# Attention, a dense FFN and routed experts on one core: moving a fourth tile's gather and transposes, and joining two short scatters

## The chip, the cores and the metric

One core of a Trainium2 chip runs the whole program in one launch. The metric is the device time of that launch in microseconds (us). Engines by the names of the profile: PE (TensorE, matmuls and transposes), PEld (its weight loads), DVE (VectorE), ACT (ScalarE), POOL (GpSimd), SP (SyncE, which here only issues transfers). ACT and POOL issue transfers too; every indirect transfer (gather or scatter by a list of row numbers) is POOL's.

## The reference

Three stages, float32 in and out:

```
x   = attention(q, k, v)            # 4 batches, 8 heads, 512 local + 32 global positions, window 32
x   = relu(x @ w_in)**2 @ w_out     # (2176, 512) -> 2048 -> 512
out = moe2(x):
    compute = x @ w_skip > 0
    e_idx   = argmax(x[compute] @ w_gate)            # one of 8 experts
    gate    = softmax(x[compute] @ w_gate)[e_idx]
    y[mask of e] = gate * (relu(x[mask] @ w1[e]) @ w2[e])   # 512 -> 1024 -> 512
    out = x, and out[compute] = x + y
```

Only the third stage bears on the change. How many tokens an expert has is known only on the chip.

## The kernel before, in words

**Routing.** While the FFN runs, `route` gives each token a slot in its expert's list. Rows of x and the gate factor are stored in `x2d` (513 numbers a row), rows of x alone in `out`. `slot_rows` (L795) makes two integer tables: `gidx`, the row to gather for each slot, and `sidx`, the row of `out` to write (out of bounds for an empty slot). A column of 128 slots is one tile; tile (e, j) is expert e's j-th.

**A tile's work.** `gather(e, j)` (L882) is an indirect DMA of 128 rows into a buffer `xg`. `prepare(e, j)` (L888) is four PE transposes (`etr`), an ACT cast and a DVE subtraction, which leave the rows transposed as a high and a low part. `expert_tile(e, j)` (L897) is a generator of nine steps. Steps 0 to 3 are the first product in two halves (L912 to L914), each followed by its relu; after each half four transposes (`ertr`). Steps 4 to 7 are the second product, two of eight slices a step (L927 to L929, 6 matmuls of 128x512 a step, 24 in all). Step 8 is a DVE operation (L950) that multiplies by the gate and adds the token rows from `xg`. Then the indirect DMA (L954) scatters the result to `out`. All scatters write `out`, and each waits until the scatter before it has landed. The result's buffer (`"xt"`) is one.

**Order.** Each engine runs its instructions in the order in which they are emitted, and so does each of the queues of SP, ACT and POOL. The last part of the FFN and the first tiles of expert 0 follow a table written by hand, `TAIL` (L41): `X` and `Y` are steps of tiles (0, 0) and (0, 1); `g02`, `g10`, `g20` are gathers; `p02` is `prepare(0, 2)`; `z1`, `z2` transpose 32 rows of experts 1 and 2; `W` and `w` fetch expert weights on ACT's and SP's queue; `N` loads counts into registers. Weights come in parts of 512 KB, eight an expert (numbers 8e to 8e + 7).

**The branches.** `more(0, 2)` (L1258) runs tile (0, 2) if expert 0 has over 256 tokens. It emits the gather of (0, 3) at its head and `prepare(0, 3)` at step 5, and then branches on 384. On these data expert 0 has between 257 and 384 tokens: (0, 3) is gathered and transposed and never used. Expert 3 has four tiles, (3, 2) and (3, 3) as a pair; `more(3, 1)` emits their gathers at its head and their transposes at steps 5 and 6.

**The short form.** Experts 1 and 2 (`FEW`) have at most 32 tokens each, so `few` is taken (L1324). `rest_tile` (L1020) computes 32 tokens with plain fp32 weights: first product (L1029), relu, transposes, second product (L1048), four DVE operations of 32x128 (L1058) into a result tile (`"xt"` for expert 1, `"x2"` for expert 2), and a scatter of 32 rows (L1063). Both run interleaved. The branch first emits on SP the weight parts 23 to 28 (`fetch_expert`, L831; 23 is the last of expert 2, 24 to 31 are expert 3's), and ACT's first work in it is the cast of part 24 (L839). A part's transfer waits for its buffer, and for the semaphore that the eighth transfer before it used. `run` (L1304) then goes through experts 3 to 7: at step 5 of an expert's first tile `prepare(e, 1)`, at step 6 (`U0`) `prepare(e + 1, 0)`; its `later` list puts expert 2's DVE operations and scatter into steps 0 and 1 of tile (3, 0). An expert's next gathers stand at steps 2 and 3 (`AHEAD`).

Of the kernel before, what the change touches and what calls it, by code (L numbers as in the profile page):

```python
# [11 lines left out]
I32 = mybir.dt.int32  # L12
# [28 lines left out]
TAIL = """  # L41
    r W r w w T T s r s T T c T s T T r T T s r C T W w s O T W T C C T T W c C T W p00 c p01 T c T X w W X w t Z t
    X w X t X Y W t X X X t S Y W X w Y g02 Y N g10 g20 Y N N Y N W W X Y N N p02 N
    Y Y W Y Y W z1 z2
"""

WARM = 8
# [7 lines left out]
def attention_ffn_routed_experts(  # L55
# [22 lines left out]
    nc = tc.nc  # L78
    B, H, SL, D = q_l.shape
    SG = q_g.shape[2]  # L80
    P = 128
    S = SL + SG
    NTOK, DM = out.shape
# [31 lines left out]
    def sb(tag, bufs, shape, name, dtype=F32):  # L115
        return spool.tile(shape, dtype, tag=tag, bufs=bufs, name=name + arm[0])
# [765 lines left out]
    def gather(e, j, gi):  # L882
        nc.gpsimd.indirect_dma_start(  # L883
            out=gathered(e, j), out_offset=None, in_=x2d, in_offset=bass.IndirectOffsetOnAxis(ap=gi, axis=0),
            bounds_check=NTOK - 1, oob_is_err=False,
        )
# [130 lines left out]
        rest[e] = rest_in[-1][:, z]  # L1017
        nc.scalar.copy(rest[e], tr[:, :, 0:SEG])

    def rest_tile(e, j, si, in_arm, o_tag):  # L1020

        x, fw = rest[e], F // NQ
        xg = gathered(e, j)[0:SEG]
        parts_in = [est[e * NPE + i] for i in range(NPE)]
        h = inner(in_arm, 0, f"eh_rest{e}")[:, 0:fw]
        for k in range(KD):
            for c in range(NQ):
                fb, at = divmod(c * fw, DM)
                nc.tensor.matmul(  # L1029
                    h[SEG * c:SEG * (c + 1), :], lhsT=x[:, k, :],  # L1030
                    rhs=parts_in[fb * (KD // 2) + k // 2][:, k % 2, at:at + fw],
                    start=(k == 0), stop=(k == KD - 1),
                )
        r = sb("sm", 2, [P, S], f"er_rest{e}")[:, 0:fw]
        nc.scalar.activation(r, h, AF.Relu)
        yield
        tr = pair(f"ertr_rest{e}")
        nz = fw // P
        for z in range(nz):
            nc.tensor.transpose(tr[:, z, :], r[:, z * P:(z + 1) * P], ident)  # L1040
        g = sb("pT", 2, [P, 4, P], f"eg_rest{e}")[:, 0:nz, :]
        nc.vector.tensor_copy(g, tr[:, 0:nz, :])
        yield
        y = ps.tile([P, DM], F32, tag="x2", bufs=2, name=f"y_rest{e}{arm[0]}")[:, 0:P]
        for f in range(KE):
            c, z = divmod(f, nz)
            for d in range(NQ):
                nc.tensor.matmul(  # L1048
                    y[SEG * d:SEG * (d + 1), :], lhsT=g[:, z, SEG * c:SEG * (c + 1)],
                    rhs=parts_in[NPE - KE // 2 + f // 2][:, f % 2, d * P:(d + 1) * P],  # L1050
                    start=(f == 0), stop=(f == KE - 1),
                )
        yield
        shape, bufs = {"xt": ([P, 3 * BLK], 1), "x2": ([P, ROW], 2)}[o_tag]
        o = sb(o_tag, bufs, shape, f"eo_rest{e}")[0:SEG, 0:DM]
        for d in range(NQ):
            cols = slice(d * P, (d + 1) * P)
            nc.vector.scalar_tensor_tensor(  # L1058
                out=o[:, cols], in0=y[SEG * d:SEG * (d + 1), :], scalar=xg[:, DM:DM + 1], in1=xg[:, cols],
                op0=ALU.mult, op1=ALU.add,  # L1060
            )
        yield
        nc.gpsimd.indirect_dma_start(  # L1063
            out=out, out_offset=bass.IndirectOffsetOnAxis(ap=si[0:SEG], axis=0), in_=o, in_offset=None,
            bounds_check=NTOK - 1, oob_is_err=False,
        )
        yield

    UNROLL = 5
# [3 lines left out]
    with tc.manual_schedule():  # L1073
# [103 lines left out]
        def slot(idx, e, j):  # L1177
            c = e * TPE + j
            return idx[:, c:c + 1]
# [13 lines left out]
        for what in TAIL.split():  # L1193
            if what == "T":
                next(ffn, None)
            elif what in "XY":
                j = "XY".index(what)
                if j not in early:
                    early[j] = expert_tile(0, j, first_slots[1][:, j:j + 1])
                next(early[j], None)  # L1200
            elif what in "rst":
                if what not in route_gens:
                    route_gens[what] = route(*outs["g"])
                next(route_gens[what])
            elif what in "Cc":
                convert_expert(converted[0], nc.vector if what == "C" else nc.gpsimd)
                converted[0] += 1
            elif what in "Ww":
                fetch_expert(fetched[0], nc.scalar if what == "W" else nc.sync)
                fetched[0] += 1  # L1210
            elif what == "O":
                open_places()
            elif what == "S":
                slot_rows(gidx, sidx, 0, NSLOT)
                nc.vector.tensor_tensor(
                    out=sizes[:, E:E + 1], in0=count[:, FEW[0]:FEW[0] + 1], in1=count[:, FEW[1]:FEW[1] + 1], op=ALU.max
                )
                nc.vector.tensor_copy(cnt, sizes)
            elif what == "N":
                load_count(to_load.pop(0))  # L1220
            elif what == "Z":
                convert_expert(converted[0], low_only=True)
            elif what[0] == "z":
                prepare_rest(int(what[1]), 0)
            elif what[0] in "gp":
                e, j = map(int, what[1:])
                if what[0] == "g":
                    gather(e, j, slot(gidx, e, j))
                else:
                    prepare(e, j)  # L1230
# [27 lines left out]
        def more(e, j):  # L1258

            if j == UNROLL:  # L1260
                with tc.For_i(UNROLL, (n_tok[e] + (P - 1)) // P, 1) as it:
                    gi = sb("gi", 2, [P, 1], f"gi{e}", I32)
                    nc.vector.tensor_copy(gi, gidx[:, bass.ds(it + e * TPE, 1)])
                    si = sb("si", 2, [P, 1], f"si{e}", I32)
                    nc.vector.tensor_copy(si, sidx[:, bass.ds(it + e * TPE, 1)])
                    gather(e, UNROLL, gi)
                    prepare(e, UNROLL)
                    for _ in expert_tile(e, UNROLL, si):
                        pass
                return  # L1270
            with tc.If(n_tok[e] > least(e, j), label=f"more{e}_{j}{arm[0]}") as branch:  # L1271
                if e and j == 4:
                    gather(e, j, slot(gidx, e, j))
                    prepare(e, j)
                    following = ()
                else:
                    following = (2, 3) if e else range(j + 1, UNROLL)[:1]
                for z in following:
                    gather(e, z, slot(gidx, e, z))
                for u, _ in enumerate(expert_tile(e, j, slot(sidx, e, j))):  # L1280
                    if u in HINTS and following:
                        hint(e, j + 1, HINTS[u])
                    if 5 <= u < 5 + len(following):
                        prepare(e, following[u - 5])
                more(e, j + 1) if j != 1 else more_two(e)
            if least(e, j) > j * P:
                with branch.Else():
                    with tc.If(n_tok[e] > j * P):
                        for _ in rest_tile(e, j, slot(sidx, e, j), True, "xt"):
                            pass  # L1290

        def more_two(e):

# [7 lines left out]
                        hint(e, 4)  # L1301
                more(e, 4)

        def run(experts, later=(), ahead=NST - 1):  # L1304
            later = list(later)
            for e in experts:
                for u, _ in enumerate(expert_tile(e, 0, slot(sidx, e, 0))):
                    if u in HINTS:
                        hint(e, 1, HINTS[u])
                    if u == U1:  # L1310
                        prepare(e, 1)
                        if e == E - 1:
                            prepare_rest(e, 1)
                    if u == U0 and e + 1 < E:
                        prepare(e + 1, 0)
                    work(e, u, ahead if e == experts[0] else NST - 1)
                    if later:
                        later.pop(0)()
                more(e, 1)
# [3 lines left out]
        shared.update((n, raws[n]) for n in est)  # L1323
        with tc.If(n_tok[E] <= SEG, label="few") as few:  # L1324
            arm[0] = "_a"
            rests = [rest_tile(e, 0, slot(sidx, e, 0), False, o) for e, o in zip(FEW, ("xt", "x2"))]
            n = AFTER * NPE
            for i in range(-1, 5):
                fetch_expert(n + i)
# [16 lines left out]
                    give(FEW[z] * NPE + i)  # L1346
            next(rests[0])
            gather(AFTER + 1, 0, slot(gidx, AFTER + 1, 0))
            next(rests[0])
            run(range(AFTER, E), [lambda: next(rests[1])] * 2, 4)  # L1350
        with few.Else():
            arm[0] = "_b"
            for kept, then in zip((est, raws), carried):
# [41 lines left out]
```

## Time and profile before

| | |
|---|---|
| median of 3 runs | 731.11 us (730.87 to 731.68) |
| the profiled execution | 732.7 us, span 731.0 us |
| mean granted clock | 0.982 |
| PE busy | 692.2 us, 95% |
| DVE, ACT, POOL busy | 398.2, 369.3, 166.8 us |
| DMA | 95.31 MB, mean 130 GB/s |

How to read it: the routed part with which the change deals begins about 560 us into the span. PE is busy nearly everywhere, so the view that matters is who ends PE's few idle stretches. In a timeline a row is start, length, engine, line, operation, output<-inputs, shapes, count, and in brackets the engine's idle time before it with what ended it. A row of a table of windows is start:end, length, busy time of PE, PEld, DVE, ACT and POOL, the granted clock as a share of full speed, the busy share of the 16 DMA engines (it can come out a little over 1), and GB/s.

### The profile page before, as it was taken

Reading aid. Unit: us, or ns where it says so; the run is one execution under the profiler, and the core shown is the slowest. Engines: PE = TensorE matmul, PEld = TensorE weight load, DVE = VectorE, ACT = ScalarE, POOL = GpSimd, SP = SyncE. Lnnn points to the kernel's source line nnn. Section 1 sums busy time; section 2 is a strip of 40 time slices with the busy share of each in tenths; the row PEclk is TensorE's granted clock in tenths of the full one; section 3 lists DMA queues with packets and bytes.
Section 4 is the critical chain, followed back from the end, with each engine's and each line's share of the span. In section 5 each row is a group of like instructions: output and inputs, shape, how many; then the busy total and the mean of one; then the engine's idle time right before and its main releaser. Section 6 shows DMA issues by size and latency. Waiting matters only on the chain. (4 is left out here: it accounts for less than half of the span.)

```text
span 731.0 us, 18725 instructions
## 1 busy us (share of the span) xinstructions
PE 692.2 (95%) x7613; PEld 576.4 (79%) x7613; DVE 398.2 (54%) x1065; ACT 369.3 (51%) x943; POOL 166.8 (23%) x210
## 2 busy tenths in 40 slices
PE   6789998999999999999999999999999979799994
PEld 3566677889888988988888988888878858697773
DVE  2879955853653364465256265533387228226992
ACT  5757567665544554535455453544345226215880
POOL 5000043462112222112121221222204312302211
PEclk9699999999999999999999999999999999999999
DMA  9999552063054304042711204100266959805910
GB/s 275 252 280 308 187 144 46 4 169 78 18 125 118 75 31 113 2 98 65 170 35 35 73 2 157 39 22 31 75 205 213 280 211 356 320 15 181 346 40 23
DMA packets 119129, 95.31 MB, mean 130 GB/s; under 512 B 84853, under 2 KB 92021, under 8 KB 119012
## 3 DMA queue, kind: packets, MB, share of 16 engines
q1 hardware_dynamic: 108304, 71.01, 34.6%
q10 hardware_dynamic: 8292, 15.48, 6.4%
q0 software_dynamic: 2416, 7.28, 3.0%
q8 instruction: 71, 1.16, 0.7%
q14 instruction: 46, 0.38, 0.2%
HBM read 81.49 MB, written 12.79 MB: 129 GB/s over the span
## 5 line engine op out<-in xcount | busy, mean ns | idle before, releaser
L184 POOL TENSOR_TENSOR gl<-g,gh 128x256 fp32r<-128x256 f32 x107 | 79.5, 743 | 303.0 <-ACT gh L183 153.6
L700 PE MATMUL h<-xh,w_in 128*128 128x256 f32 x464 | 134.8, 291 | 0.7 <-ACT xh L183 0.7
L701 PE MATMUL h<-xl,w_in 128*128 128x256 f32 x464 | 129.5, 279 | 0.3 <-DVE xl L184 0.3
L702 PE MATMUL h<-xh,w_in 128*128 128x256 f32 x464 | 129.6, 279 | 0.0
L725 PE MATMUL acc<-w_out,gh 128*128 128x512 f32 x232 | 97.6, 421 | 1.5 <-ACT gh L183 1.5
L727 PE MATMUL acc<-w_out,gl 128*128 128x512 f32 x232 | 91.9, 396 | 0.4
L726 PE MATMUL acc<-w_out,gh 128*128 128x512 f32 x232 | 91.6, 395 | 0.0
L700 PEld LDWEIGHTS h<-xh,w_in 128*128 128x128 f32 x464 | 87.1, 188 | 4.2 <-ACT xh L183 0.9
L701 PEld LDWEIGHTS h<-xl,w_in 128*128 128x128 f32 x464 | 87.2, 188 | 2.6 <-DVE xl L184 0.5
L704 ACT ACTIVATE g<-h 128x256 f32<-128x256 f32 x128 | 48.7, 380 | 78.1 <-PE h L702 45.4
L702 PEld LDWEIGHTS h<-xh,w_in 128*128 128x128 f32 x464 | 87.1, 188 | 0.1
L433 ACT ACTIVATE sm<-sm,mx 128x128 f32<-128x128 f32 x120 | 46.7, 390 | 50.1 <-DVE mx L431 50.1
L741 DVE TENSOR_TENSOR g<-h,g 128x256 f32<-128x256 f32 x53 | 22.2, 419 | 85.7 <-ACT g L704 85.7
L183 ACT CAST gh<-g 128x256 fp32r<-128x256 f32 x116 | 47.2, 407 | 42.0 <-DVE g L741 40.0
L727 PEld LDWEIGHTS acc<-w_out,gl 128*128 128x128 f32 x232 | 43.5, 188 | 12.3 <-POOL gl L184 1.8
L725 PEld LDWEIGHTS acc<-w_out,gh 128*128 128x128 f32 x232 | 43.6, 188 | 8.6 <-ACT gh L183 1.9
L726 PEld LDWEIGHTS acc<-w_out,gh 128*128 128x128 f32 x232 | 43.8, 189 | 5.7
L426 DVE TENSOR_TENSOR sm<-sc,mask 128x512 f32<-128x512 f32 x30 | 20.6, 687 | 23.8 <-PE sc L413 23.0
L255 POOL TENSOR_TENSOR w_in<-st_raw_in,w_in 128x512 fp32r<-128x512 f32 x10 | 13.0, 1308 | 81.5 <-ACT w_in L251 81.5
L413 PEld LDWEIGHTS sc<-kT,qT 64*32 64x32 f32 x2048 | 25.1, 108 | 6.5 <-issue 5.4
L413 PE MATMUL sc<-kT,qT 64*32 64x32 f32 (+1 forms) x2048 | 27.6, 228 | 2.0 <-issue 2.0
L883 POOL DMA_INDIRECT xg<-x2d,slots x16 | 20.5, 1282 | 39.1 <-DVE slots L800 13.1
(667 smaller groups left out, 1484.5 us busy)
## 6 DMA issues: line engine op xcount, KB each, us to landing
st_e<-in_moe_w_dram SPq DMA_DIRECT2D x46, 512.0 KB
vr<-in_v_l_dram SPq DMA_DIRECT2D x49, 192.0 KB
st_raw_in<-in_moe_w_in_dram SPq DMA_DIRECT2D x16, 512.0 KB
st_raw_out<-in_moe_w_out_dram SPq DMA_DIRECT2D x16, 512.0 KB
st_e<-in_moe_w_dram ACTq DMA_DIRECT2D x12, 512.0 KB
x2d<-x ACTq DMA_DIRECT2D x19, 256.5 KB
st_gv<-in_v_l_dram SPq DMA_DIRECT2D x8, 512.0 KB
out_dram<-x ACTq DMA_DIRECT2D x16, 256.0 KB
```

Of the source, the lines that this page charges most:

```text
L183: nc.scalar.copy(hi, src)
L184: (lo_engine or nc.vector).tensor_tensor(out=lo, in0=src, in1=hi.bitcast(F32), op=ALU.subtract)
L413: nc.tensor.matmul(scs[g][SEG * i:SEG * (i + 1), p, cols], lhsT=q[rows, p, SEG * i:SEG * (i + 1)], rhs=kT[b][rows, p, keys], start=True, s ...
L433: nc.scalar.activation(sm[:, hh, :], sm[:, hh, :], AF.Exp, bias=mx[:, hh:hh + 1], scale=SCALE, accum_out=osum[:, 2 * hh + g:2 * hh + g + 1],)
L700: nc.tensor.matmul(h, lhsT=wh, rhs=xh[:, k, :], start=(k == 0), stop=False)
L701: nc.tensor.matmul(h, lhsT=wh, rhs=xl[:, k, :], start=False, stop=False)
L702: nc.tensor.matmul(h, lhsT=wl, rhs=xh[:, k, :], start=False, stop=(k == KD - 1))
L704: nc.scalar.activation(g, h, AF.Relu)
L725: nc.tensor.matmul(acc[z], lhsT=gh[:, c], rhs=wh, start=first_one, stop=False)
L726: nc.tensor.matmul(acc[z], lhsT=gh[:, c], rhs=wl, start=False, stop=False)
L727: nc.tensor.matmul(acc[z], lhsT=gl[:, c], rhs=wh, start=False, stop=last_one)
L741: nc.vector.tensor_tensor(out=square, in0=h, in1=g, op=ALU.mult)
```

## The change

The gather of (0, 3) leaves `more(0, 2)` and stands in `TAIL` as `g03`, ahead of the last steps of tile (0, 1), and is issued whether or not there is such a tile. For expert 0 `prepare` of the next tile moves from step 5 to step 8. The short form's two results go into two halves of one 64-row tile and out in one scatter; the second list of row numbers is copied by DVE in `TAIL` (`v`) and shifted to partitions 32 to 63 by a DMA on SP at the head of the short form. In `run`, `prepare(4, 0)` moves from step 6 to step 8 of tile (3, 0).

```diff
 TAIL:
-    Y Y W Y Y W z1 z2
+    Y Y W g03 v Y Y W z1 z2

+    def scatter_rest(o, si):
+        nc.gpsimd.indirect_dma_start(
+            out=out, out_offset=bass.IndirectOffsetOnAxis(ap=si, axis=0), in_=o, in_offset=None,
+            bounds_check=NTOK - 1, oob_is_err=False,
+        )
+
-    def rest_tile(e, j, si, in_arm, o_tag):
+    def rest_tile(e, j, in_arm, o):
...
-        shape, bufs = {"xt": ([P, 3 * BLK], 1), "x2": ([P, ROW], 2)}[o_tag]
-        o = sb(o_tag, bufs, shape, f"eo_rest{e}")[0:SEG, 0:DM]
...
-        yield
-        nc.gpsimd.indirect_dma_start(
-            out=out, out_offset=bass.IndirectOffsetOnAxis(ap=si[0:SEG], axis=0), in_=o, in_offset=None,
-            bounds_check=NTOK - 1, oob_is_err=False,
-        )
         yield
...
+            elif what == "v":
+                second_si = sb("hi_i", 2, [P, 1], "si_second", I32)[0:SEG]
+                nc.vector.tensor_copy(second_si, slot(sidx, FEW[1], 0)[0:SEG])
...
                 for z in following:
-                    gather(e, z, slot(gidx, e, z))
+                    if (e, z) != (0, 3):
+                        gather(e, z, slot(gidx, e, z))
...
-                    if 5 <= u < 5 + len(following):
-                        prepare(e, following[u - 5])
+                    first = 5 if e else 8
+                    if first <= u < first + len(following):
+                        prepare(e, following[u - first])
...
-        def run(experts, later=(), ahead=NST - 1):
+        def run(experts, later=(), ahead=NST - 1, late=U0):
...
-                    if u == U0 and e + 1 < E:
+                    if u == (U0 if e != experts[0] else late) and e + 1 < E:
                         prepare(e + 1, 0)
...
-            rests = [rest_tile(e, 0, slot(sidx, e, 0), False, o) for e, o in zip(FEW, ("xt", "x2"))]
+            both_o = sb("xt", 1, [P, 3 * BLK], "eo_few")[0:2 * SEG, 0:DM]
+            both_si = sb("hi_i", 2, [P, 1], "si_few", I32)[0:2 * SEG]
+            rests = []
+            for z, e in enumerate(FEW):
+                rests.append(rest_tile(e, 0, False, both_o[z * SEG:(z + 1) * SEG]))
+            nc.vector.tensor_copy(both_si[0:SEG], slot(sidx, FEW[0], 0)[0:SEG])
+            nc.sync.dma_start(both_si[SEG:2 * SEG], second_si)
...
             gather(AFTER + 1, 0, slot(gidx, AFTER + 1, 0))
-            next(rests[0])
-            run(range(AFTER, E), [lambda: next(rests[1])] * 2, 4)
+            run(range(AFTER, E), (lambda: next(rests[1]), lambda: scatter_rest(both_o, both_si)), 4, 8)
```

What the change makes of the order on two engines. POOL, the end of `TAIL`, before (`xg1_0` holds tiles (0, 1) and (0, 3), `xg0_0` and `xg1_1` tiles (3, 0) and (3, 1); `eo_0_1` is the result of (0, 1)):

```order
L954 DMA out_0_dram<-eo_0_1_8426,s0_2478 2176x512
L883 DMA xg0_0_7727<-x2d_69,slots_7788 128x513
L883 DMA xg1_1_8018<-x2d_69,slots_7788 128x513
L1271 COMPARE_AND_BRANCH
L883 DMA xg1_0_7731<-x2d_69,slots_7788 128x513
L954 DMA out_0_dram<-eo_0_2_8538,slots_7788 2176x512
```

and now:

```order
L883 DMA xg1_0_7731<-x2d_69,slots_7788 128x513
L954 DMA out_0_dram<-eo_0_1_8426,s0_2478 2176x512
L883 DMA xg0_0_7727<-x2d_69,slots_7788 128x513
L883 DMA xg1_1_8018<-x2d_69,slots_7788 128x513
L1273 COMPARE_AND_BRANCH
L954 DMA out_0_dram<-eo_0_2_8533,slots_7788 2176x512
```

The gather of (0, 3) moved from behind the branch to ahead of the scatter of (0, 1) and the two gathers of expert 3.

POOL in the short form and the head of tile (3, 1), before (`xg0_1` is tile (4, 0), `xg0_2` (5, 0), `xg1_0` (4, 1), `xg2_0` and the last `xg0_0` (3, 2) and (3, 3)):

```order
L883 DMA xg0_1_8016<-x2d_69,slots_7788 128x513
...
L1063 DMA out_0_dram<-eo_rest1_a_8975,slots_7788 2176x512
...
L1063 DMA out_0_dram<-eo_rest2_a_9008,slots_7788 2176x512
...
L883 DMA xg0_2_8017<-x2d_69,slots_7788 128x513
...
L883 DMA xg1_0_7731<-x2d_69,slots_7788 128x513
...
L954 DMA out_0_dram<-eo_3_0_a_9135,slots_7788 2176x512
L1271 COMPARE_AND_BRANCH
L883 DMA xg2_0_8019<-x2d_69,slots_7788 128x513
```

and now:

```order
L883 DMA xg0_1_8016<-x2d_69,slots_7788 128x513
...
L1021 DMA out_0_dram<-eo_few_a_8832,si_few_a_8833 2176x512
...
L883 DMA xg0_2_8017<-x2d_69,slots_7788 128x513
...
L883 DMA xg1_0_7731<-x2d_69,slots_7788 128x513
...
L954 DMA out_0_dram<-eo_3_0_a_9129,slots_7788 2176x512
L1273 COMPARE_AND_BRANCH
...
L883 DMA xg2_0_8019<-x2d_69,slots_7788 128x513
```

One scatter stands where two stood; the rest keeps its order.

SP at the head of the short form, now, with the semaphores that each transfer waits for (before, the first row was not there and the others followed each other in the same order):

```order
L1338 DMA si_few_a_8833<-si_second_8433 32x1 [waits DMAHW7_49,DVE_49]
L831 DMA st_e23_a_8836<-in_moe2_w2_dram 128x2x512 [waits DMAHW0_49]
L831 DMA st_e24_a_8838<-in_moe2_w1_dram 128x2x512 [waits DMAHW1_49,PE_49]
L831 DMA st_e25_a_8840<-in_moe2_w1_dram 128x2x512 [waits DMAHW2_49,Pool_49]
L831 DMA st_e26_a_8842<-in_moe2_w1_dram 128x2x512 [waits DMAHW3_49,Pool_49]
L831 DMA st_e27_a_8844<-in_moe2_w1_dram 128x2x512 [waits DMAHW4_49]
L831 DMA st_e28_a_8846<-in_moe2_w2_dram 128x2x512 [waits DMAHW5_49,PE_49]
```

The small DMA stands ahead of all weight parts and is the only one of them that waits for DVE. On PE, the four transposes of (0, 3) moved from between the second product's 12th and 13th matmul of tile (0, 2) to behind its 24th.

## Rows read from the trace of the kernel before

**Rows 1.** Who ended PE's waits, 560 to 731 us: total, times, longest, in us.

```profile
PE etr L280 <- DMA xg<-x2d,slots: 4.2, 1, 4.2
PE etr_a L280 <- DMA xg<-x2d,slots: 3.8, 1, 3.8
```

**Rows 2.** Windows: busy time (x instructions) by engine, PE's granted clock, DMA share, GB/s.

```profile
585.00:590.00 5.00, 5.00 (x28) 4.06 (x26) 1.10 (x2) 1.77 (x3) 2.40 (x3) 1.00 1.05 397
...
594.50:598.50 4.00, 3.95 (x13) 3.23 (x14) 0.69 (x1) 0.58 (x1) 0.00 (x0) 0.58 0.03 7
...
635.00:639.50 4.50, 4.50 (x17) 3.71 (x18) 1.06 (x2) 1.17 (x2) 0.00 (x0) 0.62 0.30 109
```

**Rows 3.** Timeline of PE, expert 0's third tile and the head of the short form.

```profile
589.93 0.40 PE L929 MATMUL y<-e5h,ehl 128*128 128x512 f32 x1
...
594.55 0.63 PE L280 MATMUL etr<-ident,xg 128*128 128x128 f32 x4 [4.22 <-DMA xg<-x2d,slots]
...
594.93 0.63 PE L927 MATMUL y<-e6h,ehl 128*128 128x512 f32 x1
...
599.12 0.40 PE L929 MATMUL y<-e7h,ehl 128*128 128x512 f32 x1
...
600.20 1.07 PE L1029 MATMUL eh_rest_a<-st_e,x_rest 128*32 128x256 f32 x16 [0.68 <-PEq L1271]
```

**Rows 4.** Timeline of POOL, gathers (L883) and scatters (L954, L1063).

```profile
574.46 1.03 POOL L954 DMA_INDIRECT out_dram<-eo,s  x1 [0.30 <-issue]
...
583.02 1.00 POOL L954 DMA_INDIRECT out_dram<-eo,s  x1 [7.54 <-DVE eo L950]
...
587.01 1.00 POOL L883 DMA_INDIRECT xg<-x2d,slots  x1 [0.30 <-issue]
...
612.33 2.22 POOL L1063 DMA_INDIRECT out_dram<-eo_rest_a,slots  x1 [0.31 <-issue]
...
620.68 1.32 POOL L1063 DMA_INDIRECT out_dram<-eo_rest_a,slots  x1 [6.13 <-DVE xp L184]
...
627.15 1.02 POOL L954 DMA_INDIRECT out_dram<-eo_a,slots  x1 [1.87 <-DMA out_dram<-eo_rest_a,slots]
...
628.47 1.02 POOL L883 DMA_INDIRECT xg<-x2d,slots  x1 [0.31 <-issue]
```

**Rows 5.** Timeline of PE, expert 3: second product of its first and second tile.

```profile
618.52 0.47 PE L927 MATMUL y_a<-e30h_a,ehl_a 128*128 128x512 f32 x1
...
621.82 0.39 PE L912 MATMUL eh_a<-e24h_a,xp 128*128 128x512 f32 x1
...
634.95 0.63 PE L280 MATMUL etr_a<-ident,xg 128*128 128x128 f32 x4 [3.84 <-DMA xg<-x2d,slots]
...
635.33 0.48 PE L927 MATMUL y_a<-e30h_a,ehl_a 128*128 128x512 f32 x1
...
640.22 0.28 PE L970 MATMUL eph_a<-xp,e24h_a 128*128 128x256 f32 x1
```

**Rows 6.** Timeline of DVE and ACT, results of four tiles and the first cast.

```profile
581.99 0.75 DVE L950 SCALAR_TENSOR_TENSOR eo<-y,xg 128x512 f32<-128x512 f32 x1 [1.76 <-DMA out_dram<-eo,s]
...
599.79 1.05 ACT L839 CAST e24h_a<-st_e_a 128x1024 fp32r<-128x1024 f32 x1 [3.99 <-PEq L1271]
...
611.16 1.47 DVE L1058 SCALAR_TENSOR_TENSOR eo_rest_a<-y_rest_a,xg 32x128 f32<-32x128 f32 x4
...
622.99 0.74 DVE L950 SCALAR_TENSOR_TENSOR eo_a<-y_a,xg 128x512 f32<-128x512 f32 x1
```

**Rows 7.** Timeline of SP's and ACT's queue, weight parts issued.

```profile
573.49 0.92 SPq L831 DMA_DIRECT2D st_e_a<-in_moe_w_dram  x2
...
576.66 1.23 ACTq L831 DMA_DIRECT2D st_e<-in_moe_w_dram  x2
...
585.34 0.37 SPq L831 DMA_DIRECT2D st_e_a<-in_moe_w_dram  x1
```

**Rows 8.** The gathers' tile `xg`, from issue to landing.

```profile
DMA to landing us min/median/max: 3.5/7.1/7.5
```

More of the change, by code (lines that the diff above doesn't have):

```diff
@@ L1288, in more @@
                     with tc.If(n_tok[e] > j * P):
-                        for _ in rest_tile(e, j, slot(sidx, e, j), True, "xt"):
+                        o = sb("xt", 1, [P, 3 * BLK], f"eo_rest{e}")[0:SEG, 0:DM]
+                        for _ in rest_tile(e, j, True, o):
                             pass
+                        scatter_rest(o, slot(sidx, e, j)[0:SEG])
         def more_two(e):
```

## The prediction

> **What bounds the kernel now.** TensorE (PE) is busy 95% of the span, so I first asked what it waits for in the routed part, the only part that the change touches. Two waits stand out [rows 1]: transposes that sit between two groups of matmuls and wait for a gathered tile of token rows, 4.2 us and 3.8 us. Each costs more than its length: in the stretch behind the first the granted clock is 0.58, behind the second 0.62, against 1.00 ahead of the first [rows 2]. These are means of PE's two levels, 1.2 and 2.4 GHz: PE had idled for 4 us just before, and then runs mostly at the lower one. So the two places are worth more than 8 us, and the question for each edit is whether it takes one of them away and what is late instead.
>
> The first place, in PE's order of time [rows 3]: expert 0's third tile, second product, is half done at 589.93 us; the transposes of the fourth tile start at 594.55; the twelve matmuls left run from 594.93, the last starts at 599.12; the short form starts at 600.20. On these data there is no fourth tile: behind the twelve matmuls stands the short form, not another product. So PE waits 4.22 us for rows that nobody uses. Why they come late shows on GpSimd [rows 4]: the scatter of the second tile at 583.02, then three gathers, ours last at 587.01; PE goes on 7.5 us later.
>
> The second place [rows 5]: in expert 3's second tile the transposes of its third tile, 634.95, after 3.84 us of idling. On GpSimd [rows 4] that gather is issued at 628.47, behind the scatter of expert 3's first tile at 627.15. This scatter waited 1.87 us for the landing of the second short scatter (620.68), which I read as having waited for the first (612.33) in the same way, 8.35 us: all scatters write the output, and each waits for the last. The product that goes out at 627.15 was ready at 622.99 + 0.74 = 623.73 [rows 6]. So 3.4 us of the lateness are two short scatters in a row.
>
> **Edit 1: the gather goes first, its transposes last.** In the new order the gather stands before the second tile's scatter. It overwrites rows that the second tile's product still reads, and that ends at 582.74 [rows 6]. So it goes at about 583.0, 4.0 us earlier, and with 7.5 us lands at 590.5. The transposes now stand behind the twelve matmuls. Those start where PE stopped, at 590.2. At the full clock twelve such matmuls and one group of transposes took 3.30 us (618.52 to 621.82 [rows 5]); without the transposes' 0.38 (594.55 to 594.93) that is 2.92, or 0.243 each. They end at 593.1, and the rows are there 2.6 us earlier. Gains: the wait, 4.22; the slow clock, eleven steps in 4.19 us (594.93 to 599.12) against 11 x 0.243 = 2.68, so 1.51. Given back: the transposes end the tile, and the last 0.25 of their 0.63, which the next matmul covered, lie open. Net **5.5**.
>
> What is the gather moved past? The second tile's scatter and two gathers of expert 3 each go one step of GpSimd's queue later, 1.33 us (587.01 - 583.02 in three steps). The scatter must land before VectorE writes the third product at 593.1: issued at 584.3 and 7.5 us under way it lands at 591.8. Expert 3's rows are wanted after the short form has begun, 9 us behind their issue at 585.7. Both are covered; of the moved gather, what lands after 593.1 costs its lateness one for one.
>
> **Edit 2: the small copy on SP's queue.** To scatter both results at once, the second list of 32 row numbers must move to partitions 32 to 63: VectorE copies it, and a DMA on SP shifts it. SP runs far ahead of the compute engines: it issued the short form's weight transfers from 573.49 on [rows 7]. Now they stand behind this DMA, which waits for the copy, which stands behind the second tile's product: 582.8. So five 512 KB transfers slide by up to 9.3 us. Who needs them? ScalarE's first cast of expert 3, 599.79 now [rows 6], 594.3 then. Its transfer is the second, out at about 584.0 (0.4 to 0.5 us of issue each). Its flight is not shown; the bounds are 3.5 us, the quickest gather [rows 8], and 8.7 us: a transfer issued by ScalarE's queue at 576.66 holds back SP's fifth until 585.34 [rows 7], since its semaphore is used again eight transfers later. I take the long end, because the DMA engines are full there (share 1.05 [rows 2]): 592.7, 1.6 us early. The casts of the others follow one by one behind that. Cost 0. The sixth waits for PE's branch and moves with it. The two copies of 32 numbers on VectorE are bounded by 0 and the 0.75 us of a full product [rows 6]; the engine idles 1.76 us ahead of that product and nothing of PE's hangs on it there: 0.
>
> **Edit 3: one scatter for both results.** It can go when the second result is done, 611.16 + 1.47 = 612.6 [rows 6], in times of before (all of this moves forward by 5.5). A 32-row scatter took 8.35 us, the 128-row one at 574.46 some 7.5 (the product at 581.99 waited for it [rows 4, 6]); 64 rows land by about 621.0. Expert 3's first product overwrites them and is due at 622.3: 1.3 us to spare. Its scatter follows at 623.4, and the gather for the third tile at about 624.7 instead of 628.47. PE wants the rows at 631.1 (634.95 - 3.84). The flight was 6.5 there, 7.5 at the long end, so they land at 631.2 to 632.2. But the two gathers in between, which flew just ahead of it, now go some 7 us earlier (GpSimd was free for them from 622.0, then from 612.6 + 2.2), which speaks for the short end. I take a rest of 0.2 us, with 1.1 as the far end. Gain: 3.84, and the slow clock behind it, 4.89 us (635.33 to 640.22) against 3.30 for the same work one tile earlier [rows 5], so 1.59; less 0.2: **5.2**.
>
> A rule speaks differently. The Trainium skill, "DMA: Bandwidth & Descriptors", section on the anatomy of one DMA of GpSimd's path, puts such a DMA at about 2.0 us plus its bytes at 436 GB/s; for 128 rows of 513 numbers that is an estimate of 2.6 us. By it the rest would be nothing and the sum 10.9. The trace has 7.5 and 6.5 for such gathers, so I do not use it.
>
> **Edit 4: transposes of expert 4's first tile two steps later**, in expert 3's first tile. PE does the same work; only the point at which the rows are wanted moves back. 0.
>
> **Sum.** 5.5 + 5.2 = 10.7. The profiled execution took 732.7 us around a span of 731.0, and would take 722.0. It stands 1.6 above the median of the runs, 731.11, so I forecast **720.4 us**. The weight stream and all tiles behind move along.
>
> **Rivals.**
> (a) *Only the first stall goes.* The joint scatter, or the gather behind it, lands late, so that PE idles 3 us or more and the clock falls again. For it: the DMA engines are full, and margins of 1.3 and 0 us stand in a row. Against: the gather leaves 3.8 us earlier whatever its flight. Price 4 to 5.2: 724.4 to 725.6. Chance 0.15.
> (b) *The first gather goes first and is still not home*, so that edit 1 does not do what it says: five weight transfers leave in the same microseconds. From rows: 2.6 MB at 397 GB/s [rows 2] are 6.6 us; behind all of them the gather would land at 583 + 6.6 + 1 = 590.6, still early; it must be over 10 us under way to matter. All of edit 1 lost gives 725.9. Chance 0.05. The Trainium skill, same page, section "Issuing engines are not separate DMA queues", has all issuers share 16 engines: by that rule the sharing is real, and the full share in the trace agrees.
> (c) *Slower: SP's chain becomes the bound.* The other half of the tile that the small DMA fills is written by VectorE at the head of the short form. If the DMA waits for that copy, SP is held until about 594.6, the second transfer leaves at 595.5 and lands at 599.0 to 604.2. ScalarE's casts, and PE behind them, are 4.7 to 9.9 late, with 1.6 for the clock, and five transfers (6.6 us) stand in front of the stream that feeds experts 3 and 4. At the long end 720.4 + 11.5 = 731.9, with the stream 738.5. Slower by over 0.2% once the first cast waits more than 10.6 us. Against: what the DMA reads is the early copy, 12 us sooner. Chance 0.04.
> (d) *Nothing measurable*: (c) at its long end without the stream, or (a) and (b) together: 730 to 732. Chance 0.03.
>
> **Numbers.** The forecast has 0.73; its own range is 719.2 to 721.8 (a rest of 0 to 1.1, and what the flights leave open). The range 719.2 to 725.8 adds (a); about 1 in 10 is left out. 0.2% is 1.5 us, about what a measurement of this kernel can tell from no change: faster 0.93, same 0.03, slower 0.04.
>
> **What would show it.** Right: no wait of PE for a gather above 1.1 us; the four transposes behind the twelve matmuls; a clock near 1.00 in both stretches; the short form starting near 594.7; one scatter from it, and expert 3's third-tile gather 3 to 4 us sooner against its tile; SP's first short-form transfer near 583. Wrong: ScalarE's first cast of expert 3 waiting for its transfer, or PE idle for 3 us or more ahead of either group of transposes.

## The result and the profile after

The changed kernel takes **719.55 us** (median of 4 runs, 719.21 to 719.95), the kernel before 731.39 beside it (730.87 to 732.9): a ratio of 0.9835, 95% interval 0.9818 to 0.9852. The forecast was 720.4, range 719.2 to 725.8. The gain is 11.8 us where 10.7 was forecast.

| profiled execution | before | after |
|---|---|---|
| time / span, us | 732.7 / 731.0 | 719.74 / 718.0 |
| mean granted clock | 0.982 | 0.991 |
| PE busy, us | 692.2 (95%) | 689.4 (96%) |
| first matmul of tile (0, 2) to the short form, us | 19.38 | 13.36 |
| short form to the first matmul of the pair, us | 40.02 | 34.44 |
| pair to the end of the span, us | 90.78 | 90.26 |

The first of these three stretches holds the first wait, the second the second wait. Before, they run from 580.82 to 600.20 [rows 3], from there to 640.22 [rows 5], and to 731.0. They are the measure in all that follows: the place at which tile (0, 2) starts moves by 2.3 us between profiles of kernels that are the same up to there (579.18 to 581.52), and that lies in every total. The stretches come from one profile of each kernel. Where no wait for a gather lies in them they agree closely (the first is 13.36 in five profiles); where one does, they do not: the first stretch of before is 19.38, and 20.46 in number 4, which has the same code there.

PE after the change. The matmuls follow each other, the transposes of (0, 3) stand behind the last, and the short form's line is now L1035:

```profile
579.94 0.50 PE L912 MATMUL eh<-e0h,xp 128*128 128x512 f32 x1
...
589.04 0.39 PE L929 MATMUL y<-e5h,ehl 128*128 128x512 f32 x1
589.27 0.40 PE L927 MATMUL y<-e6h,ehl 128*128 128x512 f32 x1
...
591.79 0.39 PE L929 MATMUL y<-e7h,ehl 128*128 128x512 f32 x1
592.02 0.60 PE L280 MATMUL etr<-ident,xg 128*128 128x128 f32 x4
593.30 3.01 PE L1035 MATMUL eh_rest_a<-st_e,x_rest 128*32 128x256 f32 x52 [0.69 <-ACTq L1273]
...
624.08 0.60 PE L280 MATMUL etr_a<-ident,xg 128*128 128x128 f32 x4
...
627.74 0.28 PE L970 MATMUL eph_a<-xp,e24h_a 128*128 128x256 f32 x1
```

Against [rows 3]: 589.93 to 594.93 was 5.00 us and is 0.23 (589.04 to 589.27); the eleven steps to the last matmul were 4.19 and are 2.52. The transposes at 624.08 have no bracket: nothing idles ahead of them, where [rows 5] has 3.84.

The four longest of the six things that PE waits for from 560 to 718 us, in total, times, longest (the other two are 0.4 and 0.2). Neither row of [rows 1] is left:

```profile
PE eh_rest_a L1035 <- ACTq L1273: 0.7, 1, 0.7
PE y_rest_a L1054 <- DVE eg_rest_a L1048: 0.6, 1, 0.6
PE ertr_rest_a L1046 <- ACT er_rest_a L1041: 0.6, 1, 0.6
PE eh_a L912 <- PEq L1273: 0.4, 1, 0.4
```

Windows, columns as in [rows 2]: the granted clock is the full one in every stretch where it had been 0.58 and 0.62.

```profile
590.00:592.00 2.00, 2.00 (x10) 1.61 (x9) 0.00 (x0) 0.00 (x0) 0.00 (x0) 1.00 1.04 402
593.30:600.00 6.70, 6.53 (x136) 4.92 (x140) 4.04 (x7) 4.94 (x7) 0.98 (x1) 1.00 0.93 316
600.00:628.00 28.00, 28.00 (x204) 23.07 (x194) 18.57 (x27) 13.90 (x20) 10.33 (x7) 1.00 1.04 388
```

POOL, for [rows 4]:

```profile
573.69 1.02 POOL L954 DMA_INDIRECT out_dram<-eo,s  x1 [0.30 <-issue]
580.46 1.03 POOL L883 DMA_INDIRECT xg<-x2d,slots  x1 [5.75 <-DVE si_second L1220]
581.80 1.02 POOL L954 DMA_INDIRECT out_dram<-eo,s  x1 [0.30 <-issue]
...
606.01 1.79 POOL L1021 DMA_INDIRECT out_dram<-eo_few_a,si_few_a  x1 [0.88 <-DVE eo_few_a L1062]
...
616.42 1.03 POOL L954 DMA_INDIRECT out_dram<-eo_a,slots  x1 [4.94 <-DVE eo_a L950]
617.76 1.02 POOL L883 DMA_INDIRECT xg<-x2d,slots  x1 [0.31 <-DMA xg<-x2d,slots]
```

The gather of (0, 3) is at 580.46, 0.52 behind the start of tile (0, 2); it was 6.19 behind it. One scatter leaves the short form, 12.71 behind its start, and tile (3, 0)'s scatter now waits for its own result (DVE), not for a landing. The gather for (3, 2) comes 24.46 behind the short form's start, before 28.27: 3.8 us sooner, as the prediction wanted (3 to 4).

SP, and the first cast, for [rows 6, 7]. First SP:

```profile
580.26 0.60 SPq L1338 DMA_DIRECT2D si_few_a<-si_second  x1
580.92 12.18 SPq L831 DMA_DIRECT2D st_e_a<-in_moe_w_dram  x6
```

and ACT:

```profile
593.72 1.04 ACT L839 CAST e24h_a<-st_e_a 128x1024 fp32r<-128x1024 f32 x1 [0.48 <-ACTq L1273]
```

SP's weight parts start 7.4 us later than before (8.3 against the start of tile (0, 2), where up to 9.3 was forecast), and the cast waits for the branch (ACT's sequencer) and not for its part.

### The profile page after: what moved, and what is told of

Same layout as the page of the kernel before. It is cut to its first block, busy times and chain, and to the rows that moved or that the text cites. A ratio compares the mean times of both kernels' runs of the same rounds, so it can differ in the third digit from the quotient of the medians.

```text
span 718.0 us, 18725 instructions
## 1 busy us (share of the span) xinstructions
PE 689.4 (96%) x7613; PEld 575.8 (80%) x7613; DVE 398.7 (56%) x1067; ACT 369.8 (52%) x943; POOL 165.1 (23%) x209
## 4 chain that ended last, share of the span: by engine, by line
PE 70%; DMA 17%; issue 5%; DVE 3%; SPq 1%; ACT 1%; POOL 1%; POOLq 0%; ACTq 0%; DVEq 0%
DMA xg<-x2d,slots 15%; PE h L700 8%; PE acc L725 7%; PE acc L727 7%; PE h L702 7%; PE h L701 7%; PE acc L726 7%; PE sc L413 3%; PE acc L723 3%; PE h L697 3%; PE po L451 2%; PE ptr L442 2%; PE gsa L485 1%; PE qtr L341 1%; PE x2tr L280 1%
## 5 line engine op out<-in xcount | busy, mean ns | idle before, releaser
L184 POOL TENSOR_TENSOR gl<-g,gh 128x256 fp32r<-128x256 f32 x107 | 79.5, 743 | 303.1 <-ACT gh L183 146.1
L883 POOL DMA_INDIRECT xg<-x2d,slots x16 | 20.0, 1250 | 42.8 <-DVE slots L800 13.1
L743 ACT ACTIVATE g<-g 128x256 f32<-128x256 f32 x63 | 26.2, 417 | 4.5 <-ACT g L704 2.5
```

The source lines that it names most:

```text
L184: (lo_engine or nc.vector).tensor_tensor(out=lo, in0=src, in1=hi.bitcast(F32), op=ALU.subtract)
L743: nc.scalar.activation(square, g, AF.Square)
```

## The experiments

Each ran beside the kernel before on the same chip. "First stretch" and "second stretch" are the two rows of the table above, from the experiment's own profile. The medians are of 4 to 7 runs that spread over 1.7 to 6.7 us, and those of numbers 1, 2, 4, 5 and 6 lie 0.2 to 0.9 outside the times expected of them; the readings below rest on the stretches and the waits.

**1. Edit 1 alone.** The kernel before with

```diff
-    Y Y W Y Y W z1 z2
+    Y Y W g03 Y Y W z1 z2
```

and the two edits of `more` (no gather of (0, 3) at the head, `first = 5 if e else 8`).

> The kernel before with edit 1 alone (the fourth tile's gather first, its transposes last). Theory (each edit takes away one of PE's two waits, and they add up): 5.5 to 6.0 us off, 725.4 to 725.9, the second wait of 3.8 us stays with its slow clock behind it. Rival (one cause behind both, or a shift that is given back later): either nearly all 11.8 us, or under 4 us because expert 3's gathers then meet the weight stream in another way.

Measured: 726.51 us beside 733.17, ratio 0.9922 (0.9888 to 0.9956). First stretch 13.36, as in the changed kernel to the last digit; second 40.24, against 40.02 before. The second wait stands where it was, 4.1 us, behind two short scatters. POOL:

```profile
573.10 1.02 POOL L954 DMA_INDIRECT out_dram<-eo,s  x1 [0.30 <-issue]
584.18 1.03 POOL L883 DMA_INDIRECT xg<-x2d,slots  x1 [10.07 <-DVE eo L950]
...
604.84 2.21 POOL L1063 DMA_INDIRECT out_dram<-eo_rest_a,slots  x1 [0.30 <-issue]
613.48 1.02 POOL L1063 DMA_INDIRECT out_dram<-eo_rest_a,slots  x1 [6.43 <-DVE xp L184]
...
619.81 1.03 POOL L954 DMA_INDIRECT out_dram<-eo_a,slots  x1 [2.04 <-DMA out_dram<-eo_rest_a,slots]
```

So edit 1 is worth 6.02 us against this profile of before, and 7.1 against the first stretch of number 4; it brings nothing behind the short form. That holds although the gather leaves only at 584.18.

**2. Edits 2, 3 and 4 without edit 1.** The changed kernel with

```diff
-    Y Y W g03 v Y Y W z1 z2
+    Y Y W v Y Y W z1 z2
```

and `more` as before.

> The changed kernel without edit 1: gather and transposes of the fourth tile where they were, the joint scatter, the small DMA on SP and the later transposes of expert 4 kept. Theory: 5.2 to 5.6 us off, 725.8 to 726.2, the first wait of 4.2 us stays. With SP's transfers held for 10 us the first gather could land sooner (rival: the held transfers, not the order, take part of the first wait away): then the first wait is under 3 us and the time under 724.5.

Measured: 725.07 us beside 733.17, ratio 0.9881 (0.9832 to 0.993). Second stretch 34.50: the second wait is gone without edit 1. First stretch 18.25, 1.13 better than before; its wait is 3.1 us. DVE writes the product of (0, 1) without a wait, where [rows 6] has 1.76 us for the first scatter's landing, and the gather of (0, 3), two steps behind it in POOL's queue, leaves 4.51 behind the start of tile (0, 2) (584.84) and not 6.19.

```profile
579.82 0.75 DVE L950 SCALAR_TENSOR_TENSOR eo<-y,xg 128x512 f32<-128x512 f32 x1
580.49 0.13 DVE L1220 COPY si_second<-slots 32x1 int32<-32x1 int32 x1
```

The small DMA holds back SP's weight parts until 581.32 here, and without them beside it the first scatter is home sooner (number 3 undoes the hold alone, and the wait is back). So the hold of edit 2 does help the first gather to leave sooner. What that is worth in time is not shown: the 1.13 is no more than the first stretch differs by between two profiles of the same code (19.38 and 20.46). With edit 1 nothing of it is left (number 3).

**3. No hold.** The changed kernel with the small DMA behind the weight parts:

```diff
-            nc.sync.dma_start(both_si[SEG:2 * SEG], second_si)
             for i in range(-1, 5):
                 fetch_expert(n + i)
+            nc.sync.dma_start(both_si[SEG:2 * SEG], second_si)
```

> The changed kernel with the small DMA on SP behind the six weight parts instead of ahead of them, so that nothing is held. Theory (holding the transfers costs and gains nothing): within 0.5 us of the changed kernel's 719.6; SP's first short-form transfer back near 573, the second tile's product again waiting about 2 us for the first scatter's landing, with no wait of PE. Rival (the hold frees the DMA engines for the gathers): PE waits for a gather again, 1 us or more slower.

Measured: 719.98 us (718.98 to 721.32), ratio 0.9823 (0.9774 to 0.9872); stretches 13.43 and 34.60, against 13.36 and 34.44. DVE waits for the first scatter again:

```profile
581.39 0.75 DVE L950 SCALAR_TENSOR_TENSOR eo<-y,xg 128x512 f32<-128x512 f32 x1 [2.18 <-DMA out_dram<-eo,s]
```

The gather of (0, 3) leaves at 582.41, 2.72 behind the start of tile (0, 2) (579.69) and so 2.2 later there than in the changed kernel, and no row of PE waits for it. (What ends the wait of the short form's first matmul is now a weight part, 0.76, where it was the branch, 0.69.) Edit 2 at nothing holds in the whole change.

**4. One scatter fewer, nothing else.** The kernel before with

```diff
-            run(range(AFTER, E), [lambda: next(rests[1])] * 2, 4)
+            run(range(AFTER, E), [lambda: next(rests[1])], 4)
```

> The kernel before without the scatter of expert 2's 32 rows (those rows of the output stay as they were); nothing else differs, so no small DMA, no 64-row tile, no later transposes. Theory (the second wait comes from two short scatters in a row, each waiting for the last): the second wait goes and 4.9 to 5.6 us with it, 725.6 to 726.4, as in the run with the joint scatter alone. Rival (the later transposes of expert 4 or the held transfers took it away): the wait of 3.8 us stays in most part, over 728.

Measured: 726.82 us beside 733.17, ratio 0.9907 (0.9877 to 0.9937). Second stretch 35.36, 4.66 better than before, of 5.58 that the change gives there. (The first is 20.46, 1.1 worse than before, with a wait of 4.6. The edit does not touch it, so this much is difference between profiles.) Of the second wait 0.8 is left:

```profile
PE etr L280 <- DMA xg<-x2d,slots: 4.6, 1, 4.6
...
PE etr_a L280 <- DMA xg<-x2d,slots: 0.8, 1, 0.8
```

The second short scatter in the chain is thus most of the second wait; the last 0.8 is not a matter of the scatters in a row (number 7 shows of what).

**5. Gather first, transposes in the middle.** The changed kernel with

```diff
-                    first = 5 if e else 8
-                    if first <= u < first + len(following):
-                        prepare(e, following[u - first])
+                    if 5 <= u < 5 + len(following):
+                        prepare(e, following[u - 5])
```

> The changed kernel with the fourth tile's transposes back at step 5, the gather still first. Theory (what counts is the gather's lead): the gather leaves near 580.5, the transposes are wanted near 589.3, 8.8 us later, against flights of up to 7.9 us so far: no wait over 0.5 us, 719.3 to 720.1. Rival (the transposes' place is what counts): PE waits 1 us or more there.

Measured: 718.37 us beside 732.72 (717.97 to 720.98), ratio 0.9803 (0.9774 to 0.9833); stretches 13.41 and 34.54. No wait: the gather leaves at 582.04, PE reaches the transposes at 590.88. (The profiled execution is the slowest of the four, 720.98.)

**6. Transposes last, gather where it was.** The changed kernel with `g03` taken out of `TAIL` and the gather back at the head of `more(0, 2)`.

> The changed kernel with the fourth tile's gather back behind the branch, the transposes still last. Theory: the gather leaves near 584.8 and is 7.5 to 7.9 us under way, wanted near 592.1: a wait of 0.2 to 0.7 us and no fall of the clock, 719.8 to 720.4, so either half of edit 1 would have done nearly alone. Rival (the gather's place counts): a wait of 2 us or more and the slow clock behind it, over 722.5.

Measured: 720.64 us, ratio 0.9831 (0.9797 to 0.9865); stretches 13.91 and 34.55. PE's wait is

```profile
593.52 0.63 PE L280 MATMUL etr<-ident,xg 128*128 128x128 f32 x4 [0.37 <-DMA xg<-x2d,slots]
```

for a gather of 585.44, 8.1 us under way. So, beside edits 2 to 4, either half of edit 1 takes away all or nearly all of the first wait. With the transposes last they are wanted twelve matmuls later (2.75 us, 589.27 to 592.02 in the changed kernel), and PE's granted clock is 1.00 there (590 to 594). Neither half was run alone without edit 2, with which these gathers leave sooner.

**7. Edit 4 undone.** The changed kernel with

```diff
-scatter_rest(both_o, both_si)), 4, 8)
+scatter_rest(both_o, both_si)), 4)
```

> The changed kernel with the transposes of expert 4's first tile back at step 6. The prediction put this edit at 0. New theory, from the run that left one scatter out: with them at step 6 VectorE does their subtraction (0.7 us) ahead of expert 3's first product, so the scatter and the third tile's gather go 0.7 us later and PE waits 0.3 to 0.8 us: 719.9 to 720.6. By the prediction: no wait, 719.3 to 719.9.

Measured: 720.55 us, ratio 0.9845 (0.9798 to 0.9892); stretches 13.36 and 35.29, the second 0.85 longer than with edit 4. (The times alone, 718.46 to 724.45 in four runs, do not tell the two kernels apart.) A wait is back at the transposes of (3, 2), 624.90, 0.68 us. Where it comes from is DVE's order. Here:

```profile
613.13 1.22 DVE L845 TENSOR_TENSOR e32l_a<-st_e,e32h_a 128x1024 fp32r<-128x1024 f32 x1
614.35 0.69 DVE L184 TENSOR_TENSOR xp<-etr_a,xp 128x512 fp32r<-128x512 f32 x1
614.95 1.21 DVE L845 TENSOR_TENSOR e33l_a<-st_e,e33h_a 128x1024 fp32r<-128x1024 f32 x1
616.09 0.74 DVE L950 SCALAR_TENSOR_TENSOR eo_a<-y_a,xg 128x512 f32<-128x512 f32 x1
```

and in the changed kernel:

```profile
613.13 1.22 DVE L845 TENSOR_TENSOR e32l_a<-st_e,e32h_a 128x1024 fp32r<-128x1024 f32 x1
614.26 1.22 DVE L845 TENSOR_TENSOR e33l_a<-st_e,e33h_a 128x1024 fp32r<-128x1024 f32 x1
615.40 0.75 DVE L950 SCALAR_TENSOR_TENSOR eo_a<-y_a,xg 128x512 f32<-128x512 f32 x1
616.06 0.68 DVE L184 TENSOR_TENSOR xp<-etr_a,xp 128x512 fp32r<-128x512 f32 x1
```

`prepare(4, 0)` ends in a DVE subtraction (L184). At step 6 it stands ahead of the product of (3, 0), on which that tile's scatter hangs and behind it the gather of (3, 2); at step 8 it stands behind. The whole chain moves by 0.69 us: product 616.09 and 615.40, gather 618.44 and 617.76.

**8. The rival on the slower side, made real.** The changed kernel with the copy of the second list in the short form instead of `TAIL`, so that SP's small DMA waits for a copy at the head of the short form:

```diff
-    Y Y W g03 v Y Y W z1 z2
+    Y Y W g03 Y Y W z1 z2
...
+            second_si = sb("hi_i", 2, [P, 1], "si_second", I32)[0:SEG]
+            nc.vector.tensor_copy(second_si, slot(sidx, FEW[1], 0)[0:SEG])
             nc.sync.dma_start(both_si[SEG:2 * SEG], second_si)
```

> The changed kernel with the second list's copy at the head of the short form instead of behind the second tile, so that SP's small DMA and all weight parts behind it wait until about 594: the prediction's slower rival made real. By its price ScalarE's first cast of expert 3 starts 4.7 to 9.9 us late and the clock costs 1.6: 725.9 to 731.1; with the stream late as well up to 738. If the weights had more room than that price says: under 724.

Measured: 727.75 us (726.06 to 729.29), ratio 0.9934 (0.9911 to 0.9957): 8.2 us over the changed kernel's 719.55 (from another comparison), still below the kernel before. First stretch 13.36, second 42.04, 7.60 more. SP issues its small DMA at 595.75 and the parts from 596.41. ACT's cast then stands on its part:

```profile
602.39 1.04 ACT L839 CAST e24h_a<-st_e_a 128x1024 fp32r<-128x1024 f32 x1 [8.03 <-DMA st_e_a<-in_moe_w_dram]
```

and PE behind ACT, since the relu of the short form stands behind that cast:

```profile
603.78 0.69 PE L1046 MATMUL ertr_rest_a<-ident,er_rest_a 128*128 128x128 f32 x2 [5.69 <-ACT er_rest_a L1041]
```

PE's granted clock around that wait and behind it:

```profile
600.00:606.00 6.00, 2.03 (x8) 1.43 (x8) 1.58 (x3) 3.20 (x6) 0.00 (x0) 0.57 1.00 374
606.00:612.00 6.00, 6.00 (x136) 5.28 (x135) 5.11 (x9) 2.88 (x3) 0.86 (x1) 0.86 1.05 388
```

This mechanism exists, then, and its 7.60 lies in the 6.3 to 11.5 that the prediction's price gives without the weight stream; what keeps it out of the changed kernel is that the copy stands 13 us ahead of the short form.

**9 to 11. Can the transposes go still cheaper?** Three versions, compared on one chip: the changed kernel again; the changed kernel with the transposes of (0, 3) only inside the branch that uses the tile; and number 5 again.

> The changed kernel itself, for comparison on one chip with the two versions beside it. Both theories: 719.6 us (719.2 to 720.0 earlier), 11 to 13 us below the kernel before; last matmul of the second product to the start of the short form 1.51 us as in the earlier profile.

```diff
-                    if first <= u < first + len(following):
+                    if first <= u < first + len(following) and (e, j) != (0, 2):
...
+                if (e, j) == (0, 3):
+                    prepare(0, 3)
```

> The changed kernel, but the fourth tile's transposes stand inside the branch that uses the tile, so that on these data they are not run at all. Theory: they cost what lies open at the end of the third tile, 1.51 - 1.08 = 0.43 us, plus the part of 0.38 that no later matmul covers; 0.4 to 0.8 us faster than the changed kernel, and the last matmul to the short form back near 1.08. Rival (the end of the tile is bound by the short form's own start, its branch and count): the gap stays near 1.5 and the time the same within 0.2 us.

> The changed kernel with the transposes of the fourth tile back in the middle of the second product, the gather still first; it gave 718.37 (717.97 to 720.98) beside 720 to 720.6 of its neighbours in an earlier comparison. Theory: in the middle the next matmuls cover 0.25 of the transposes' 0.63 us, so it is 0.25 to 0.5 us faster than the changed kernel. Rival (the earlier difference was scatter): within 0.2 us of the changed kernel. A gain of over 1 us would mean that the place of the transposes moves something else too, ScalarE's and VectorE's part of them in front of the short form's first casts being the first suspect.

| | median, us | ratio | first | second |
|---|---|---|---|---|
| changed again | 719.33 (718.83 to 721.91) | 0.983 (0.9809 to 0.985) | 13.36 | 34.45 |
| transposes in the branch | 718.91 (717.97 to 721.57) | 0.9827 (0.9805 to 0.9848) | 12.91 | 34.44 |
| gather first, transposes in the middle | 720.61 (719.1 to 721.87) | 0.9835 (0.9818 to 0.9852) | 13.40 | 34.44 |

Without the unused transposes the short form follows 1.07 behind the last matmul (before 1.08, after 1.51) and the first stretch is 0.45 shorter. The transposes' price is shown there, and with it the rival of number 10 falls; the times of the two kernels overlap and do not show it. The theory for number 11 falls: transposes in the middle cost as much as at the end (13.40, and 13.41 in number 5). The lower median of number 5 did not come again (720.61). Where it came from is not shown, since the profiled execution of number 5 took 720.98 and not 718.37; the edit does not touch what follows the pair, which was 89.83 there and 91.58 in number 11, against 90.26 in the changed kernel.

## Why the prediction was right

The mechanism, its places and the total were right: no wait for a gather is left, the clock is 1.00 in both stretches, the short form starts at 593.30, which is 594.18 in times of before (0.88 later there, where tile (0, 2) starts) against "near 594.7". The three stretches settle the account: 6.02 + 5.58 in the two that the change touches are 11.60; the medians differ by 11.84. The rest of the 13.0 between the two spans is 0.88 ahead of tile (0, 2) and 0.52 behind the pair, where nothing was changed.

**Edit 1: 5.5 forecast, 6.02 measured.** The wait, 4.22, and the clock were read rightly. What the sum missed: moving the transposes also frees their own slot in the middle. From 589.93 to 594.93 [rows 3] were 0.40 + 4.22 + 0.38 and now are 0.23, so 4.77 and not 4.22. The clock gave 1.67 (4.19 to 2.52) for 1.51, since the pitch of the matmuls is 0.229 us and not the 0.243 taken from expert 3. At the end 0.43 (1.51 less 1.08) was given back for 0.25. In sum 0.55 + 0.16 - 0.18 = 0.53 too little. (The wait itself differs by nearly as much between profiles of the same code, 4.22 and 4.57 in number 4.) The gather's lead was better than thought too: I let it go behind the product at 582.74, but that product's wait of 1.76 us was for the scatter's landing, which the held transfers brought forward. It left 11.6 us ahead of its transposes and was 6.8 under way, by the profile's time from issue to landing; the longest gather of that part of the run took 9.5. The scatter that it was moved past was under way 9.8 us (from 581.80) where I had 7.5, and still landed 0.6 ahead of the third product (592.22).

**Edit 2: 0 forecast.** 0 in the whole change (number 3), through margins: ACT's cast does not wait for its part, and the first gather has its lead with or without the hold. The margin was not the one worked out: the transfer of the cast's part was 10.0 us under way, over the 8.7 that I called the long end, but left at 581.8, 1.4 sooner in times of before than the 584.0 forecast, and landed some 1.9 ahead of the cast (593.72). That the hold brings the first scatter home sooner was not seen.

**Edit 3 and edit 4: 5.2 + 0 forecast, 5.58 measured, with two errors that cancel.** The step that failed is "expert 3's first product ... is due at 622.3". I had its inputs ready then, but DVE is busy until 622.99 with the subtraction of `prepare(4, 0)` and a weight part, and the row [rows 6] shows no bracket: the product already ran at once behind them. So the joint scatter alone brings the product to 22.79 behind the short form's start (616.09 - 593.30), as before (622.99 - 600.20), the gather 25.14 behind that start, where I had 24.5, and a wait of 0.68, inside my 0 to 1.1 but not the 0.2 taken. Edit 3 is worth 40.02 - 35.29 = 4.73. Edit 4, put at 0 because "PE does the same work", moves just that DVE subtraction: 615.40 - 593.30 = 22.10, my 622.3 again, and 0.85 us (35.29 - 34.44). What I left out of `prepare` was its part on DVE. That the sum of the two came out 0.4 from the forecast is in part luck.

**The two short scatters in a row** as the cause of the second wait were a reading of one bracket of 1.87 us (the second scatter's own bracket, 6.13 in [rows 4], names a DVE subtraction that the code emits only behind it; the first scatter was 7.5 us under way and landed at 619.83, 0.85 ahead of the second); number 4 shows it: leaving one out moves the scatter of (3, 0) from 26.95 to 23.80 behind the short form's start, the same place as the joint scatter without edit 4 (23.81).

**The rivals.** (a) did not happen, but it was near. In number 7 PE could take up the rows 6.46 us after their issue (618.44 to 624.90). In the changed kernel they are wanted 6.32 us after it (617.76 to 624.08), and no wait shows. The gather was 6.1 us under way there, so some 0.2 us of margin is left. (b) did not happen: the lead was 11.6 us, the flight 6.8. (c), put at 731.9 or 738.5, was priced by number 8: 7.60 in its stretch. The first cast started 7.96 behind the short form's start (602.39 - 594.43) and 0.42 in the changed kernel, so 7.5 late, in my 4.7 to 9.9. PE's wait makes 5.69 of the 7.60; the other 1.9 is near the 1.6 that I had put down for the clock. The weight stream behind it did not cost 6.6 us in addition. The 10.6 us from which on it would have been slower than before were not reached even there.

## What to carry to other kernels

A wait for data that may never be used can be removed by asking later as well as by fetching sooner; here, beside the other edits, either half nearly sufficed, so cost them apart before paying for both. Where results leave through a chain of writes to one tensor, count the links: one 64-row scatter in place of two 32-row ones was worth more than 4 us far behind it. When a piece of work is moved, list what it issues on every engine: that of the four edits which seemed worth nothing on TensorE took one VectorE operation out of the chain of the next gather.

## What was not expected of the hardware

- The first scatter's flight depends strongly on SP's weight transfers beside it. With the parts issued from 572 or 573 on it landed 7.8 us after its issue in number 3 and 7.6 in number 4, and DVE's product that waits for it started 7.53 us after its issue in the kernel before [rows 4, 6] and 10.06 in number 1 (573.10 to 583.16). With the parts held it took 4.1 in the changed kernel and 3.9 to 4.4 in the eight other profiles with the hold. How the sharing makes 7.5 in one run and 10 in another was not settled.
- A 64-row scatter in two halves was not slower than a 32-row one beside the same stream: issued at 606.01, it landed 7.1 us later, 2.3 ahead of the product at 615.40 that overwrites its rows. The 32-row scatter of 612.33 [rows 4] took 7.5.
